# A shorter prologue in a fused mLSTM and MLP-mixer kernel: 40-row products without fills, a split gate computation, and two late subtractions moved back

## The chip, the cores and the metric

The kernel runs on one core of a Trainium2 chip. The metric is the device time of one execution in microseconds (us); the time before the change is the median of three runs. A difference is later told from no change at about 0.2% of it.

## The reference

The kernel computes an mLSTM attention and feeds its output to an MLP-mixer. Shapes: 4 batches, 8 heads, 768 steps, head dimension 40, so 320 features. Cut to what matters:

```python
for t in range(S):                                     # mLSTM, per batch and head
    m_new = maximum(f[t] + m, i[t])
    f_stab, i_stab = exp(f[t] + m - m_new), exp(i[t] - m_new)
    C = f_stab * C + i_stab * outer(v[t], k[t])
    n = f_stab * n + i_stab * k[t]
    y[t] = sigmoid(o[t]) * (C @ q[t]) / maximum(abs(n @ q[t]), 1)
x = y laid out as (batch, 768, 320)
u = x + (relu(x^T @ w_tok1) @ w_tok2)^T                # tokens: 768 -> 256 -> 768
out = u + relu(u @ w_ch1) @ w_ch2                      # channels: 320 -> 1536 -> 320
```

## The kernel before, in words

**Chunks.** The recurrence is computed in chunks: each batch has six chunks of 128 steps, and a unit `(b, c)` is one chunk of one batch for all eight heads. `u0`, `u1`, `u2` are the first three units of batch 0. Within a unit, `st_s` (L308) forms the products k q of every head (16 matmuls, four per head pair of tiles; keys and queries of a head lie in 40 of 64 rows of the tile `raw`, two heads one above the other), `st_p` (L319) multiplies them by the decay factors `dd` on VectorE, `st_pv` (matmuls at L442, or L411 for batches 2 and 3) multiplies them with the values, and `st_state` (from L370) adds what the state `Cst` gives (L380: state times the scaled queries `q3t`) and forms the next state: `pu` (L388) on TensorE, masked with `bm_t` (L393) and added to the decayed state (`Cn`, L397) on VectorE. The tile `raw` exists three times; `zero_rows` (L211) writes zeros once into the 24 unused rows of each 64, since the products of all units but the first read 64 rows.

**Gates.** `gates_of(c0, c1)` (L118) runs the stabiliser's scans for all batches over the chunks c0 to c1 on VectorE, then two subtractions that leave `b_t` and `phi` in the tile `z`. `split` (L175, L176) cuts `z` into bf16 pieces that TensorE spreads over 128 partitions (`spread_split`, `spread_phi`: L166, L181, L184) and over the queries' layout (`spread_q`: L199, L139, L140); ScalarE takes the exponentials (`prep_exp` L292, `prep_q3` L275), and GpSimd or VectorE multiplies the queries by their factors (`prep_q3`, L281). `prep_kw` (L304, GpSimd) scales the keys for the state. `sigmoid` (L222) and `x0_ops` (L479 to L494) finish a unit of batch 0: `x`, and its two-piece form `xh` (ScalarE) and `xl` (GpSimd) for the token GEMM.

**Order.** Nothing is scheduled automatically: each engine executes its instructions in the order in which the program issues them, and so does the queue of loads on SyncE (SP). Batch 0's attention is a prologue that takes the first 48 us or so. From then on TensorE computes the MLP of batch b, and a generator (`att`, L529) is advanced between its steps to issue the attention of batch b+1. In the MLP, `halves` computes the hidden layer of the channel GEMM: ScalarE writes `gh` (L836), VectorE the second piece `gl` (L837). Some hidden tiles lie in a list `closing`; `att` issues their `gh` and `gl` just behind `st_p`.

**Prologue.** `warm(n)` (L897) issues n matmuls on zeros. The order by hand is: loads, `gates_of(0, 2)`, the splits of chunks 0 and 1, the products of `u0`, `gates_of(2, 6)`, the mask (`state_mask`, L104), the products of `u1`, the queries of `u1`, the splits of chunk 2 (VectorE) and of chunks 3 to 5 (GpSimd), the outputs of `u0`; then a loop over c = 1 to 4 prepares unit c+1 (`n1`) and finishes unit c. Two lines of it matter below:

```python
        (nc.vector if u[0] == 1 else nc.gpsimd).tensor_tensor(q3t, q3t, pq, ALU.mult)      # prep_q3, L281
        (v if c == NC - 1 else nc.gpsimd).tensor_tensor(xl, x, f32(xh), ALU.subtract)      # x0_ops, L494
```

Of the kernel before, what the change touches and what calls it, by code (L numbers as in the profile page):

```python
# [18 lines left out]
L = 128  # L19
# [16 lines left out]
def kernel(ctx: ExitStack, tc: tile.TileContext, gates, qk, q3, kv, og,  # L36
# [67 lines left out]
    def state_mask():  # L104
        nc.gpsimd.memset(bm_t, 1.0)
        bm4 = bm_t.rearrange("p (g i e) -> p g i e", g=3, i=3)
        for s in (1, -1):
            nc.gpsimd.affine_select(bm4, bm4, pattern=[[0, 3], [-s * D, 3], [0, E1]], compare_op=ALU.is_ge,
                                    fill=0.0, base=0 if s > 0 else D - 1, channel_multiplier=s)

    floor_b = wp.tile([128, 1], F32, name="floor_b")
    nc.gpsimd.memset(floor_b, 2.0 ** -14 - 0.5)
# [5 lines left out]
    def gates_of(c0, c1):  # L118
        lo, hi = c0 * L, c1 * L
        sl, sd = slice(lo, hi), slice(max(lo, 1), hi)  # L120
        v = nc.vector
        v.tensor_tensor_scan(m_t[:, sl], f_t[:, sl], i_t[:, sl],
                             -1e30 if lo == 0 else m_t[:, lo - 1:lo], op0=ALU.add, op1=ALU.max)
        yield
        first = f_t.rearrange("p (c t) -> p c t", t=L)[:, max(c0, 1):c1, 0]
        v.tensor_tensor(first, first,
                        m_t.rearrange("p (c t) -> p c t", t=L)[:, max(c0, 1) - 1:c1 - 1, L - 1], ALU.add)
        yield
        v.tensor_tensor_scan(phi[:, sd], rst2[:, sd.start - lo:hi - lo], f_t[:, sd],
                             m_t[:, 0:1] if lo == 0 else 0.0, op0=ALU.mult, op1=ALU.add)  # L130
        yield
        v.tensor_tensor(b_t[:, sd], i_t[:, sd], phi[:, sd], ALU.subtract)
        yield
        v.tensor_tensor(phi[:, sd], phi[:, sd], m_t[:, sd], ALU.subtract)
        yield

# [73 lines left out]

    def zero_rows(i):  # L211
        for p in (32, 96):
            t = raws[i][p:p + 32].rearrange("p a h t -> p a (h t)")
            if i == 1:
                nc.scalar.activation(t, zero[p:p + 32].unsqueeze(1).to_broadcast([32, 2, 512]), AF.Copy)
            else:
                nc.gpsimd.memset(t, 0.0)

    def sigmoid(b, r=range(2), part=slice(0, 3)):
# [51 lines left out]
    def prep_q3(u):  # L271
        if u[1] == 0:
            return
        q3t, pq = T[u]["q3"]
        nc.scalar.activation(pq, T[u].get("psq", pq), AF.Exp)  # L275
        if "psw" in T[u]:
            cols_w0_out(T[u]["psw"], u[1])
        if u[1] < NC - 1:
            T[u]["decay"] = a = ap.tile([120, 3], F32, tag="decay", name="decay")
            nc.gpsimd.tensor_copy(a, pq[:, :, L - 1])  # L280
        (nc.vector if u[0] == 1 else nc.gpsimd).tensor_tensor(q3t, q3t, pq, ALU.mult)  # L281

# [24 lines left out]

    def st_s(u, mult=True, mid=iter(()), rows=64, pool=(ps_s, "s")):  # L308
        t = T[u]
        t["s"] = [pool[0].tile([128, 4, L], F32, tag=pool[1], name="ps_sc") for _ in range(2)]  # L310
        for h in range(4):
            for hf in range(2):
                r = t["raw"][64 * hf:64 * hf + rows]
                nc.tensor.matmul(t["s"][hf][:, h, :], r[:, 1, h, :], r[:, 0, h, :], start=True, stop=True)  # L314
        if mult:
            st_p(u, mid)
# [158 lines left out]
    def x0_ops(u):  # L475
# [16 lines left out]
        xh, xl = (pool.tile([128, DM], F32R, tag=a, name=a, bufs=3 if pool is sp else 2) for a in ("xh", "xl"))  # L492
        nc.scalar.activation(xh, x, AF.Copy)
        (v if c == NC - 1 else nc.gpsimd).tensor_tensor(xl, x, f32(xh), ALU.subtract)  # L494
        xs[u] = (x, xh, xl)
# [29 lines left out]
    def after(u, n):  # L525
        i = units.index(u) + n
        return units[i] if i < len(units) else None

    def att(b):  # L529
        for c in range(NC):  # L530
# [14 lines left out]
            st_p(u)  # L545
            while closing:
                closed.append(halves(side.pop(closing.pop())))
            if n2 and not ahead:
# [14 lines left out]
            if not th or joined(u):  # L563
                st_state(u, banks(u))
            if n1 and three(u):
                prep_mask(n1)
# [337 lines left out]

    warm(10)
    zero_rows(1)
    zero_rows(2)
    load_qk(u0, 0)
    load_qk(u0, 1)
    load_kv(u0)  # L910
    for u in us[0:3]:
        load_phi(u)
    load_qk(u1, 0)
    load_qk(u1, 1)
    load_sig(0, 0)
    q3s = {u1: load_q3t(u1)}
    load_kv(u1)
    load_sig(0, 1)

    T[u0]["phi"] = r = [spread_late(ps_h, "h") for _ in range(2)]  # L920
    warm(4)
    step(gates_of(0, 2), 9)
    split(0, 1)
    spread_phi(r, 0)
    t = ps_m.tile([128, HP], F32, tag="m", name="gw")
    cols_w0(t, 0)
    st_s(u0, mult=False, rows=D)
    split(1, 2)
# [5 lines left out]
    prep_kw(u0)  # L934
    state_mask()
    load_qk(u2, 0)
    load_qk(u2, 1)
    q3s[u2] = load_q3t(u2)
    load_kv(u2)
# [8 lines left out]
    step(gr, 9)  # L948
    zero_rows(0)
    load_phi(us[3])  # L950
    load_qk(us[3], 0)
    load_qk(us[3], 1)
    prep_q3(u1)
    prep_kw(u1)
    split(2, 3)
    split(3, NC, nc.gpsimd)
# [6 lines left out]
    st_p(u1)  # L963
    warm(1, (ps_h, "h"))
    spread_split(u2)
# [8 lines left out]
    for c in range(1, NC):  # L974
# [12 lines left out]
        if c < NC - 1:  # L987
            spread_q(n1)
            prep_q3(n1)
            prep_kw(n1)  # L990
        if c == NC - 2:
# [26 lines left out]
        if c < NC - 1:  # L1018
# [6 lines left out]
            else:  # L1025
                dec_abs(nxt[1] + 2)
        step(x0, 9)
        if c == NC - 1:
# [195 lines left out]
```

## Time and profile before

| | us |
|---|---|
| median of three runs (lowest, highest) | 424.73 (424.26, 424.93) |
| the profiled execution, its own time | 424.44 |
| its span from first to last instruction | 422.7 |
| TensorE (PE) busy | 416.2, 98% of the span |
| VectorE (DVE) busy | 277.5, 66% |
| ScalarE (ACT) busy | 185.4, 44% |
| GpSimd (POOL) busy | 143.3, 34% |
| TensorE's granted clock | 1.0 of full speed over the whole span |

Times in the rows are from the start of the span. PE is the matmuls, PEld the weight loads, which run beside them. A row of the timeline that holds several instructions has the time from the first's start to the last's end, and a bracket at its end gives idle time of the engine and what released it. The ends of matmuls are modelled and overlap the next one's start, so gaps are best read from the starts.

### The profile page before, as it was taken

The numbers are of one execution on the slowest core, as the hardware profiler recorded it, in microseconds if no ns is written. First come the engines' busy times: TensorE is split into PE (matmuls) and PEld (weight loads), VectorE is DVE, ScalarE is ACT, GpSimd is POOL, SyncE is SP. The second block draws the span as 40 slices with busy tenths as digits, with TensorE's granted clock in tenths as the row PEclk, the third lists the DMA queues.
The fourth block names the chain that finished last, engine by engine and source line by source line (L and its number), as shares of the span: only waits on it lengthen the run. The fifth ranks groups of instructions, "written<-read, shape, count | busy, mean of one in ns | idle before, by whom it ended". The sixth has DMA issues, their size and how long they took to land.

```text
span 422.7 us, 8990 instructions
## 1 busy us (share of the span) xinstructions
PE 416.2 (98%) x3507; PEld 394.4 (93%) x3507; DVE 277.5 (66%) x617; ACT 185.4 (44%) x431; POOL 143.3 (34%) x188
## 2 busy tenths in 40 slices
PE   8999999999999999999999999999999999999996
PEld 4888989999999999999999999999999999998996
DVE  7988565515868598698696698689786647111412
ACT  4977569893555544234333446234244112111211
POOL 7968488751444412142242220331450110000000
PEclk9999999999999999999999999999999999999999
DMA  7997758941777514344346122443320000000100
GB/s 202 295 299 251 259 171 289 281 142 47 241 212 229 194 34 120 107 118 132 98 151 195 48 78 57 125 116 103 111 86 33 0 32 2 0 0 2 37 27 31
DMA packets 24574, 52.34 MB, mean 124 GB/s; under 512 B 2565, under 2 KB 13325, under 8 KB 24533
## 3 DMA queue, kind: packets, MB, share of 16 engines
q1 hardware_dynamic: 24293, 51.61, 39.2%
q8 instruction: 27, 0.44, 0.4%
q10 hardware_dynamic: 240, 0.18, 0.2%
q14 instruction: 14, 0.11, 0.1%
HBM read 47.73 MB, written 4.04 MB: 122 GB/s over the span
## 4 chain that ended last, share of the span: by engine, by line
PE 93%; DVE 4%; POOL 1%; issue 1%; ACT 1%; DVEq 0%; POOLq 0%
PE acc L703 30%; PE ps_h L824 20%; PE ps_h L850 11%; PE ps_sc L314 5%; PE ps_b L703 5%; PE ps_a L703 5%; PE po L442 4%; PE po L411 3%; PE pu L388 2%; PE po L418 2%; PE po L380 2%; PE warm L897 1%; PE ps_t L771 1%; PE ps_t L770 1%; PE ps_t L769 1%; PE ps_phi L181 1%
## 5 line engine op out<-in xcount | busy, mean ns | idle before, releaser
L824 PE MATMUL ps_h<-uT,c1h 128*128 128x256 f32 x480 | 91.4, 282 | 0.0
L703 PE MATMUL acc<-c2h,gh 128*128 128x320 f32 x288 | 89.0, 318 | 0.0
L836 ACT ACTIVATE gh<-ps_h 128x512 fp32r<-128x512 f32 x48 | 28.6, 597 | 136.2 <-PE ps_h L824 111.7
L703 PE MATMUL acc<-c2l,gh 128*128 128x320 f32 x288 | 86.4, 309 | 0.0
L824 PEld LDWEIGHTS ps_h<-uT,c1h 128*128 128x128 f32 x480 | 75.8, 188 | 0.5
L824 PE MATMUL ps_h<-uT,c1l 128*128 128x256 f32 x256 | 66.1, 281 | 0.0
L703 PE MATMUL acc<-c2h,gl 128*128 128x320 f32 x288 | 61.8, 309 | 0.0
L837 DVE SCALAR_TENSOR_TENSOR gl<-ps_h,gh 128x512 fp32r<-128x512 f32 x48 | 33.0, 688 | 41.8 <-ACT gh L836 41.5
L703 PEld LDWEIGHTS acc<-c2h,gh 128*128 128x128 f32 x288 | 54.1, 188 | 1.4
L703 PEld LDWEIGHTS acc<-c2l,gh 128*128 128x128 f32 x288 | 54.2, 188 | 0.9
L854 DVE SCALAR_TENSOR_TENSOR gl<-ps_h,gh 128x512 fp32r<-128x512 f32 x24 | 16.6, 692 | 49.1 <-ACT gh L853 49.1
L824 PEld LDWEIGHTS ps_h<-uT,c1l 128*128 128x128 f32 x256 | 48.3, 189 | 0.0
L461 POOL TENSOR_TENSOR sig<-sig,ht 128x320 f32<-128x320 f32 x18 | 14.7, 818 | 98.7 <-DVE ht L422 90.6
L703 PEld LDWEIGHTS acc<-c2h,gl 128*128 128x128 f32 x288 | 47.2, 188 | 0.0
L295 ACT ACTIVATE dd<-dd,bcol 128x128 f32<-128x128 f32 x144 | 45.8, 392 | 1.4 <-POOL dd L285 1.3
L850 PE MATMUL ps_h<-uT,c1h 128*128 128x512 f32 x120 | 36.0, 394 | 0.0
L324 DVE TENSOR_TENSOR dd<-ps_sc,dd 128x512 f32<-128x512 f32 x48 | 30.9, 682 | 7.6 <-PE ps_sc L314 7.5
L512 POOL TENSOR_TENSOR xl<-x,xh 128x320 fp32r<-128x320 f32 x18 | 15.8, 876 | 51.2 <-DVE xh L510 49.8
L853 ACT ACTIVATE gh<-ps_h 128x512 fp32r<-128x512 f32 x24 | 14.3, 594 | 41.2 <-PE ps_h L850 41.2
L314 PE MATMUL ps_sc<-raw 64*128 64x128 f32 (+1 forms) x384 | 26.1, 281 | 0.0
L850 PEld LDWEIGHTS ps_h<-uT,c1h 128*128 128x128 f32 x120 | 22.1, 188 | 3.9
L314 PEld LDWEIGHTS ps_sc<-raw 64*128 64x128 f32 (+1 forms) x384 | 22.9, 188 | 2.5 <-issue 0.8
(154 smaller groups left out, 862.0 us busy)
## 6 DMA issues: line engine op xcount, KB each, us to landing
dd<-phi_d SPq DMA_DIRECT2D x18, 512.0 KB
wst<-in_wc_dram SPq DMA_DIRECT2D x22, 384.0 KB
kvt<-in_kv_dram SPq DMA_DIRECT2D x24, 324.0 KB
raw<-in_qk_dram SPq DMA_DIRECT2D x48, 160.0 KB
sig<-in_og_dram SPq DMA_DIRECT2D x8, 480.0 KB
out_dram<-x SPq DMA_DIRECT2D x24, 160.0 KB
q3t<-in_q_dram SPq DMA_DIRECT2D x20, 180.0 KB
wst<-in_wt_dram SPq DMA_DIRECT2D x8, 384.0 KB
```

Of the source, the lines that this page charges most:

```text
L295: nc.scalar.activation(dd[:, h, :], dd[:, h, :], AF.Exp, bias=bcol[:, c, HP * b + h:HP * b + h + 1])
L314: nc.tensor.matmul(t["s"][hf][:, h, :], r[:, 1, h, :], r[:, 0, h, :], start=True, stop=True)
L324: nc.vector.tensor_tensor(dd, t["s"][hf], dd, ALU.mult)
L442: nc.tensor.matmul(o, t["dd"][:, ROW[h], :], x, start=c == 0 and h == 0, stop=h == H - 1)
L461: nc.gpsimd.tensor_tensor(sg, sg, ht[:, :, 0:D], ALU.mult)
L512: nc.gpsimd.tensor_tensor(xl, x, f32(xh), ALU.subtract)
L703: nc.tensor.matmul(ps, a, m, start=(first and i == 0), stop=(last and i == n - 1))
L824: nc.tensor.matmul(ps[:, j, :], c1[x][:, a:a + 128], u[:, y, :], start=not opened and part is first and i == 0 and (order == 0 and not clo ...
L836: nc.scalar.activation(gh, ps, AF.Relu)
L837: nc.vector.scalar_tensor_tensor(gl, ps, 0.0, f32(gh), op0=ALU.max, op1=ALU.subtract)
L850: nc.tensor.matmul(ps, c1[x][:, a:a + 128], u[:, :, y, :], start=n == 0, stop=n == len(todo) - 1)
L854: nc.vector.scalar_tensor_tensor(gl, ps, 0.0, f32(gh), op0=ALU.max, op1=ALU.subtract)
```

## The change

1. `st_s` reads 40 rows of each half of `raw` instead of 64, for every unit. `zero_rows` is gone with its six fills (two on ScalarE, four on GpSimd).
2. `state_mask` is issued at the very start of GpSimd's work instead of behind `kw` of `u0`.
3. `warm(4)` becomes `warm(2)`, and the `warm(1)` ahead of the pieces of `u2` is gone.
4. The two subtractions of the gates leave `gates_of` and become `gates_end(c0, c1)`. For chunks 2 to 5 they are issued in two portions: chunk 2 alone, then the split of chunk 2, then the product of `u1`'s queries and factors (now on VectorE), then chunks 3 to 5.
5. Loads: the value load of `u0` goes behind both halves of `raw` of `u1` and the first gate load `sig`; the second `sig` load goes behind both halves of `raw` of `u2`.
6. `x0_ops` yields between `xh` and `xl`. In the loop's pass c = 4 the subtraction `xl` of unit 3 is issued behind the queries' product of unit 5.
7. In `att`, for batches 2 and 3 and c = 0 or 1, the tiles in `closing` are finished behind `prep_p3` and `st_state` instead of behind `st_p`.

The diff, cut to its core:

```diff
+    state_mask()
     floor_b = wp.tile([128, 1], F32, name="floor_b")
...
-        v.tensor_tensor(b_t[:, sd], i_t[:, sd], phi[:, sd], ALU.subtract)
-        yield
-        v.tensor_tensor(phi[:, sd], phi[:, sd], m_t[:, sd], ALU.subtract)
-        yield
+
+    def gates_end(c0, c1):
+        sd = slice(max(c0 * L, 1), c1 * L)
+        nc.vector.tensor_tensor(b_t[:, sd], i_t[:, sd], phi[:, sd], ALU.subtract)
+        nc.vector.tensor_tensor(phi[:, sd], phi[:, sd], m_t[:, sd], ALU.subtract)
...
-        (nc.vector if u[0] == 1 else nc.gpsimd).tensor_tensor(q3t, q3t, pq, ALU.mult)
+        (nc.vector if u[0] == 1 or u == u1 else nc.gpsimd).tensor_tensor(q3t, q3t, pq, ALU.mult)
...
-                r = t["raw"][64 * hf:64 * hf + rows]
+                r = t["raw"][64 * hf:64 * hf + D]
...
         nc.scalar.activation(xh, x, AF.Copy)
+        yield
         (v if c == NC - 1 else nc.gpsimd).tensor_tensor(xl, x, f32(xh), ALU.subtract)
...
             st_p(u)
-            while closing:
-                closed.append(halves(side.pop(closing.pop())))
+            if b == 1 or c > 1:
+                close()
...
                 st_state(u, banks(u))
+            close()
...
     warm(10)
-    zero_rows(1)
-    zero_rows(2)
     load_qk(u0, 0)
     load_qk(u0, 1)
-    load_kv(u0)
...
     load_sig(0, 0)
+    load_kv(u0)
     q3s = {u1: load_q3t(u1)}
     load_kv(u1)
-    load_sig(0, 1)
...
-    warm(4)
+    warm(2)
     step(gates_of(0, 2), 9)
+    gates_end(0, 2)
...
     prep_kw(u0)
-    state_mask()
     load_qk(u2, 0)
     load_qk(u2, 1)
+    load_sig(0, 1)
...
     st_p(u0)
     step(gr, 9)
-    zero_rows(0)
...
+    gates_end(2, 3)
+    split(2, 3)
     prep_q3(u1)
     prep_kw(u1)
-    split(2, 3)
+    gates_end(3, NC)
     split(3, NC, nc.gpsimd)
...
     st_p(u1)
-    warm(1, (ps_h, "h"))
     spread_split(u2)
...
             prep_q3(n1)
+            if c == 4:
+                step(x0, 9)
             prep_kw(n1)
...
-        step(x0, 9)
+        step(x0, 2 if c == 3 else 9)
```

**GpSimd at the start of the prologue.** `sel` is the last piece of the selection matrices, `kw` the scaled keys of `u0` and then of `u1`, `z` the split of chunks 3 to 5. Before:

```order
L102 COPY sel_128<-id_126 128x360
L112 MEMSET floor_b 128x1
L217 MEMSET raw_137 32x1024 x2
L304 TENSOR_TENSOR kw<-kvt,wcol 128x320
L105 MEMSET bm_t 120x369
L108 AFFINE_SELECT bm_t<-bm_t 120x369 x2
L217 MEMSET raw_135 32x1024 x2
L280 COPY decay<-pq 120x3
L281 TENSOR_TENSOR q3t<-q3t,pq 120x384
L304 TENSOR_TENSOR kw<-kvt,wcol 128x320
L175 TENSOR_TENSOR z<-z 9x2x384
```

And now:

```order
L102 COPY sel_128<-id_126 128x360
L105 MEMSET bm_t 120x369
L108 AFFINE_SELECT bm_t<-bm_t 120x369 x2
L113 MEMSET floor_b 128x1
L298 TENSOR_TENSOR kw<-kvt,wcol 128x320
L274 COPY decay<-pq 120x3
L298 TENSOR_TENSOR kw<-kvt,wcol 128x320
L177 TENSOR_TENSOR z<-z 9x2x384
```

The fills and the query product are gone from this engine, and the mask stands ahead of the first `kw`.

**VectorE between the products of `u0` and the output of `u0`** (`dd` is `st_p` of `u0`, `z` the scan, the subtractions and the split, `po` the output of `u0`). Before:

```order
L324 TENSOR_TENSOR dd<-ps_sc,dd 128x512 x2
L129 SCALAR_TENSOR_TENSOR z<-rst,f_t 36x512
L132 TENSOR_TENSOR z<-i_t,z 36x512
L134 TENSOR_TENSOR z<-z,m_t 36x512
L175 TENSOR_TENSOR z<-z 9x2x128
L176 TENSOR_TENSOR z<-z 9x2x128
L479 TENSOR_TENSOR po<-po,sig 128x8x40
```

And now:

```order
L318 TENSOR_TENSOR dd<-ps_sc,dd 128x512 x2
L130 SCALAR_TENSOR_TENSOR z<-rst,f_t 36x512
L136 TENSOR_TENSOR z<-i_t,z 36x128
L137 TENSOR_TENSOR z<-z,m_t 36x128
L177 TENSOR_TENSOR z<-z 9x2x128
L178 TENSOR_TENSOR z<-z 9x2x128
L275 TENSOR_TENSOR q3t<-q3t,pq 120x384
L136 TENSOR_TENSOR z<-i_t,z 36x384
L137 TENSOR_TENSOR z<-z,m_t 36x384
L473 TENSOR_TENSOR po<-po,sig 128x8x40
```

The split of chunk 2 moves up by most of the subtractions, and three instructions stand between it and the output of `u0`.

**VectorE in unit (2, 1)**, the first of two such places (the second is unit (3, 1); `r` and `p` are the second and third pieces of the products, `pu` and `Cn` the state). Before:

```order
L324 TENSOR_TENSOR dd<-ps_sc,dd 128x512 x2
L837 SCALAR_TENSOR_TENSOR gl<-ps_h_2409,gh 128x512
L343 TENSOR_TENSOR r<-dd 128x512 x2
L351 TENSOR_TENSOR p_2459<-r 128x512 x2
L393 TENSOR_TENSOR pu<-pu,bm_t 120x246
L393 TENSOR_TENSOR pu<-pu,bm_t 80x82
L397 SCALAR_TENSOR_TENSOR Cn<-Cn,decay,pu 120x123 x2
L397 SCALAR_TENSOR_TENSOR Cn<-Cn,decay,pu 80x82
L837 SCALAR_TENSOR_TENSOR gl<-ps_h_2444,gh 128x512
```

And now:

```order
L318 TENSOR_TENSOR dd<-ps_sc,dd 128x512 x2
L337 TENSOR_TENSOR r<-dd 128x512 x2
L345 TENSOR_TENSOR p_2447<-r 128x512 x2
L387 TENSOR_TENSOR pu<-pu,bm_t 120x246
L387 TENSOR_TENSOR pu<-pu,bm_t 80x82
L391 SCALAR_TENSOR_TENSOR Cn<-Cn,decay,pu 120x123 x2
L391 SCALAR_TENSOR_TENSOR Cn<-Cn,decay,pu 80x82
L837 SCALAR_TENSOR_TENSOR gl<-ps_h_2401,gh 128x512
L837 SCALAR_TENSOR_TENSOR gl<-ps_h_2436,gh 128x512
```

The first `gl` now stands behind `Cn`, next to the second. TensorE's order is unchanged in the whole program but for the three `warm` matmuls.

## Rows read from the trace of the kernel before

**Rows 1.** The page's part 1: busy time, share and instructions of TensorE.

```profile
PE 416.2 (98%) x3507; PEld 394.4 (93%) x3507; DVE 277.5 (66%) x617; ACT 185.4 (44%) x431; POOL 143.3 (34%) x188
```

**Rows 2.** Waits of PE and PEld: who waited for whom, us in total, times, longest.

```profile
PE po L411 <- DVE Cn L397: 0.7, 2, 0.4
...
PEld po L380 <- POOL q3t L281: 0.6, 1, 0.6
```

**Rows 3.** Timeline of PE, 6 to 26 us: start, us, engine, line, operation.

```profile
6.49 1.40 PE L897 MATMUL warm<-zero 128*128 128x512 bf16 x4
7.72 0.39 PE L181 MATMUL ps_phi<-z,id 128*128 128x128 bf16 x4
...
15.00 0.38 PE L897 MATMUL warm<-zero 128*128 128x512 bf16 x1
15.22 0.38 PE L166 MATMUL ps_phi<-late_b,id_b 128*128 128x512 bf16 x1
16.29 0.39 PE L181 MATMUL ps_phi<-z,id 128*128 128x128 bf16 x4 [0.69 <-DVE z L176]
...
18.57 0.38 PE L199 MATMUL ps_q<-z,sel 128*120 128x128 bf16 x3
...
25.55 0.77 PE L388 MATMUL pu<-kvt,kw 128*120 128x123 f32 x6
```

**Rows 4.** Groups by line and form, PE: the products; busy us, mean ns.

```profile
L314 PE MATMUL ps_sc<-raw 64*128 64x128 f32 x368 | 24.9, 280 | 0.0
...
L314 PE MATMUL ps_sc<-raw 40*128 40x128 f32 x16 | 1.2, 285 | 0.0
```

**Rows 5.** Tile z on VectorE: duration ns min/median/max, first and last start.

```profile
L175 DVE TENSOR_TENSOR z<-z x3: 417/586/1267, 5.8 to 14.1; 9x256 f32<-9x256 f32 x3
L176 DVE TENSOR_TENSOR z<-z x3: 418/419/829, 6.4 to 15.4; 9x256 f32<-9x256 f32 x3
L132 DVE TENSOR_TENSOR z<-i_t,z x2: 415/549/683, 4.9 to 12.7; 36x255 f32<-36x255 f32 x1, 36x512 f32<-36x512 f32 x1
```

**Rows 6.** Timeline of POOL, 5 to 17 us, and at 40 us.

```profile
6.23 1.95 POOL L217 MEMSET raw<- 32x1024 f32 x2
9.18 0.72 POOL L304 TENSOR_TENSOR kw<-kvt,wcol 128x320 f32<-128x320 f32 x1 [1.01 <-ACT wcol L143]
...
10.33 1.25 POOL L108 TENSOR_SCALAR_AFFINE_SELECT bm_t<-bm_t 120x369 f32<-120x369 f32 x2
...
14.09 1.00 POOL L281 TENSOR_TENSOR q3t<-q3t,pq 120x384 f32<-120x384 f32 x1
15.06 0.90 POOL L304 TENSOR_TENSOR kw<-kvt,wcol 128x320 f32<-128x320 f32 x1
...
40.04 1.02 POOL L281 TENSOR_TENSOR q3t<-q3t,pq 120x384 f32<-120x384 f32 x1
```

**Rows 7.** Timeline of DVE, 10 to 25 us, and `q3t` at 135 us.

```profile
10.00 1.29 DVE L324 TENSOR_TENSOR dd<-ps_sc,dd 128x512 f32<-128x512 f32 x2 [0.74 <-PE ps_sc L314]
...
16.27 0.50 DVE L479 TENSOR_TENSOR po<-po,sig 128x320 f32<-128x320 f32 x1
...
24.19 0.49 DVE L488 TENSOR_TENSOR x<-po,den 128x320 f32<-128x320 f32 x1
...
134.91 0.56 DVE L281 TENSOR_TENSOR q3t<-q3t,pq 120x384 f32<-120x384 f32 x1
```

**Rows 8.** Timeline of DVE and then of PE, 173 to 179 us.

```profile
173.54 0.69 DVE L837 SCALAR_TENSOR_TENSOR gl<-ps_h,gh 128x512 fp32r<-128x512 f32 x1 [0.47 <-ACT gh L836]
...
177.37 0.80 DVE L397 SCALAR_TENSOR_TENSOR Cn<-Cn,decay,pu 120x123 f32<-120x123 f32 x3
...
178.22 0.20 PE L411 MATMUL po<-v,dd 128*128 128x82 bf16 x1 [0.35 <-DVE Cn L397]
```

**Rows 9.** Timeline of ACT, 13 to 19 us.

```profile
13.73 1.90 ACT L222 ACTIVATE sig<-sig 128x960 f32<-128x960 f32 x2
...
16.94 1.24 ACT L292 ACTIVATE dd<-ps_phi 128x512 f32<-128x512 f32 x2
```

More of the change, by code (lines that the diff above doesn't have):

```diff
@@ L209 @@
     raws = [ap.tile([128, 2, 4, L], F32, tag=f"raw{i}", name=f"raw{i}", bufs=1) for i in range(3)]
[L211 to L217, printed above, removed]
     def sigmoid(b, r=range(2), part=slice(0, 3)):
@@ L306, in prep_kw, with st_s @@
         t["kw"] = kw
-    def st_s(u, mult=True, mid=iter(()), rows=64, pool=(ps_s, "s")):
+    def st_s(u, mult=True, mid=iter(()), pool=(ps_s, "s")):
         t = T[u]
@@ L527, in after, with close @@
         return units[i] if i < len(units) else None
+    def close():
+        while closing:
+            closed.append(halves(side.pop(closing.pop())))
     def att(b):
@@ L926 @@
     cols_w0(t, 0)
-    st_s(u0, mult=False, rows=D)
+    st_s(u0, mult=False)
     split(1, 2)
```

## The prediction

> **What bounds the kernel now.** I read the busy times first: TensorE works 416.2 of 422.7 us [rows 1], so the end moves only by what TensorE no longer waits for or no longer does. Next I read whom it waits for [rows 2]. Past the start there are three such places: a state `Cn` from VectorE, twice; a query product from GpSimd in the prologue; and a split from VectorE, which the timeline shows at 16.29 us [rows 3]. That is all there is to win here, some 2.5 us. A change can also lose, by making a wait where there is none. So I cost each edit at its place, in the order of time, and then look for what is late next.
>
> The sum is made against the profiled execution, 424.44, which lies 0.29 under the median of 424.73. That is inside the spread of the runs, and I add it back at the end.
>
> **40-row products.** Before the change one unit already reads 40 rows and 23 read 64: 285 against 280 ns mean [rows 4]. The number of rows does not set the time, so 23 x 16 products cost what they did: 0. The fills stood on GpSimd (1.95 us for two [rows 6], twice) and on ScalarE, where neither engine was waited for; taking them out is worth 0 by itself. What it does is let the loads of `raw` go out without waiting for them.
>
> **Early stretch, TensorE's side.** Of the four `warm` matmuls at 6.49 two go. The one at 15.00 has its successor at 15.22, so a matmul of this form takes 0.22: the pieces of `u0` start 2 x 0.22 = 0.43 earlier than 7.72 (half of the four, (7.72 - 6.49)/2 = 0.62, is the upper bound) [rows 3]. They need the split of chunk 0, which ended at 6.44 + 0.42 = 6.86 [rows 5]. The third `warm`, 15.00 to 15.22, goes too, and with the 0.43 the pieces of `u2` could start some 0.43 + 0.22 earlier plus the whole stall in front of 16.29. TensorE would be at them at about 14.9.
>
> **Early stretch, VectorE's side.** TensorE then has VectorE as its next bound, and the question is by how much (d) VectorE's output of `u0`, at 16.27 [rows 7], shifts. From there on VectorE works without a pause up to the output `x` of `u1`, at 24.19 + 0.49 = 24.68, and TensorE's `pu` at 25.55 [rows 3, 7] overwrites a bank that `x` of `u1` reads. With 0.06 for the signal that leaves 0.81 - d for TensorE's gain in this stretch: whatever it wins before, it must wait there for `x`.
>
> The terms of d. First the rows show how VectorE and GpSimd get in each other's way: the split's first half takes 0.42 alone and 1.27 when it begins at 14.10, just behind the start of GpSimd's query product at 14.09, and it ends 0.28 behind that product's end; its second half takes 0.83 instead of 0.42 beside `kw` [rows 5, 6]. So an instruction of two SBUF inputs stands still until GpSimd's ends. Beside the fills at 6.23 the second half took its least, 0.42 [rows 5, 6].
> - The mask, moved to about 6.6, now lies beside the splits of chunks 0 and 1 and the first scan. Its two selects take 1.25 together [rows 6]. Bounds 0 (each falls in a gap) and 1.25 (VectorE stands through both); half and a little more, since one split is under way when the first select asks: +0.75.
> - `kw` of `u0` (0.72 [rows 6]) waited for ScalarE; 0.43 earlier it meets the last small addition of the gates in front of 10.00. Bounds 0 (its values, now loaded later, are not there yet) and 0.72; half: +0.35.
> - Against both stands the pause of 0.74 in front of 10.00 [rows 7], which absorbs as much: -0.74. Sum so far +0.36.
> - The query product of `u1`: 0.56 on VectorE [rows 7]: +0.59 with the gap behind it.
> - Two more subtractions. A subtraction of 512 took 0.68 and one of 255 took 0.42 [rows 5], so 0.16 is fixed: 2 x 0.16 = +0.32.
> - No query product on GpSimd beside the split, and `kw` no longer beside its second half: 1.27 + 0.83 - 2 x 0.42 = -1.26 [rows 5].
> - `kw` of `u1`, 0.90 [rows 6], comes earlier and falls on some other gate instruction: 0 to 0.7, half +0.35.
>
> d = 0.36 + 0.59 + 0.32 - 1.26 + 0.35 = **+0.36**, bounds -0.9 and +1.4 when all ends fall together. TensorE's gain in the early stretch is then 0.81 - 0.36 = **0.45**. Its ends: 1.4, where TensorE's own earliest start is the limit, and -0.6.
>
> The Trainium skill, "SBUF — State Buffer", section "Who interferes with whom", states that a VectorE instruction with two SBUF inputs contends with a GpSimd instruction that reads SBUF, not with one that only writes it, and that the later one blocks fully. The rows on the product, `kw` and the fills agree. By that rule alone this part of the change is a bad trade: fills that hinder nobody are replaced, beside the splits, by selects that read and block; with the full 1.25 in place of 0.75 d is 0.86 and the early gain nothing. The mask has no instruction of VectorE beside it in the rows that fixes the price, so I keep half.
>
> **The loads moved.** The values of `u0` go behind four loads of `raw` and one of the gates; they are first needed by `kw` of `u0` at 9.18, with slack behind it, and the term above has their being late in its lower bound. The second gate load goes behind `raw` of `u2`. Its user is the second half of the two sigmoids at 13.73, which ends at 15.63 [rows 9]; behind them on ScalarE stand the exponentials of `u2`. I take it as just in time: 0; late is a rival below.
>
> **Queries ahead of `xl`.** In front of 41.11 TensorE waited 0.57 for the product that GpSimd began at 40.04 [rows 2, 6], right behind `xl`. Now the product goes first. It can start when its factors are there, about 0.5 us earlier, and TensorE then meets the state `Cn` of `u4`, which is no earlier than before. I take **0.45**, bounds 0.1 and 0.57. `xl` now ends behind the product; it is next needed by the token GEMM soon after, with little to spare, which is the lower bound.
>
> **`gl` behind the pieces.** At 178.22 TensorE waited for `Cn`, which began at 177.37 [rows 8], and so once more a batch later, 0.7 us of wait in two times [rows 2]; with the weight load that cannot run ahead the matmuls come 0.5 later each. The 0.69 of `gl` at 173.54, and the 0.47 that VectorE idled for `gh` in front of it [rows 8], leave this chain: `Cn` comes at least 0.69 earlier, the wait was under that, so it goes. `gl` itself now ends where the second `gl` of the stretch ends, still ahead of its matmuls, which TensorE reaches only behind all of L411 and the state's products. **1.0** for the two, bounds 0.9 and 1.06. What is late next there is nothing that the rows show.
>
> **Sum.** 0.45 + 0.45 + 1.0 = 1.9 against 424.44: 422.54. With the 0.29 up to the median: **422.8 us**, 0.45% below 424.73.
>
> **Rivals.**
> 1. VectorE is not held up (the values of `u0` land late, or the selects fall in gaps): d is -0.4 or so, TensorE's early gain 1.2 and the sum 2.6: 422.1. For it speaks that nothing in the rows shows a select beside a split; against it that GpSimd's readers did block wherever they met one [rows 5]. Chance 0.21.
> 2. VectorE is held up by all of both selects and by `kw`: d of 0.85 to 1.1, early gain 0 to -0.3, sum 1.3: 423.4. This is the case that the rule of the Trainium skill on the two engines, above, makes of the selects. Half of their price stands between it and mine. Chance 0.17.
> 3. No change that can be told (a difference under 0.2%, 0.85 us): the early stretch loses its 0.6 and `xl` or the moved `gl` gives half of its gain back at a wait that the rows don't show: 424.1. Chance 0.09.
> 4. Slower, by one load: the second `sig`, now behind two more loads of `raw`, lands at X. ScalarE stands in its queue until then, and behind it are half the sigmoids (0.95), the 1.31 of its table change up to 16.94, and the first exponential of `u2` (0.62) [rows 9]; TensorE's `ps_q`, at 18.57 [rows 3], needs the bank that this frees. It comes at X + 0.95 + 1.31 + 0.62 + 0.06 = X + 2.94. Up to X = 15.6 that costs nothing; the other gains, 1.45, are eaten at X = 17.1; over 0.85 slower from X = 17.9, say 425.8. Against it speaks that the queue ahead of this load no longer waits for fills, so that all of it goes out earlier. Chance 0.04.
> 5. Forty rows lose what lets two products, one above the other, overlap: if each took twice its pitch, a unit would take about 1 us more, 23 us in all. The one unit that had 40 rows did not [rows 4]. Chance 0.02: 440 or more.
>
> My forecast has the rest, 0.47.
>
> **Range and chances.** The forecast's own bounds with ordinary ends are 422.2 to 423.4. To hold 8 in 10 the range takes in rival 1 down to an early gain of 1.4 with the upper bounds of the others (3.0: 421.7) and rival 2 and part of rival 3 up to 424.1. Faster by over 0.2% (below 423.88): forecast, rival 1 and most of rival 2, 0.83. Within: rival 3 and the rest, 0.12. Slower: rivals 4 and 5 with their neighbours, 0.05.
>
> **What would show it.** Right: the wait for the split in front of 16.29 gone, a new wait of a few tenths of us on VectorE or none near `pu` of `u2`; no wait for a query product at 41 us; no wait on `Cn` at L411, twice; 16 products of 40 rows still 1.1 us. Wrong: a wait of ScalarE on a gate load near 14 us, splits of chunk 0 or 1 of over a microsecond, or a new wait on `xl` or `gl` in the list.

## The result and the profile after

The changed kernel takes **426.85 us** (median of 8 runs, 425.42 to 428.58), the kernel before 424.17 in the same session (8 runs, 423.60 to 425.29). The ratio is 1.0061, 95% interval 1.0036 to 1.0087: 0.6% slower, where 422.8 us and 0.45% faster were forecast. The profiled execution took 425.80 us, with a span of 424.1; it is one of the quicker ones of the eight, whose mean granted TensorE clock lay between 0.988 (428.58 us) and 0.996. In the profiled execution of the kernel before it was 1.0.

TensorE is busy about as long as before [rows 1], with three matmuls fewer, so the time has to be looked for in its waits and in its clock:

```profile
PE 416.6 (98%) x3504; PEld 395.7 (93%) x3504; DVE 280.3 (66%) x620; ACT 183.1 (43%) x429; POOL 138.4 (33%) x183
```

The list of PE's waits after the change (in total, times, longest) has none of the three waits past the start that the prediction named, and a new long one:

```profile
PE ps_q L201 <- ACT dd L286: 2.7, 1, 2.7
PE warm L897 <- POOL zero L61: 1.4, 1, 1.4
PE po L405 <- DVE p L345: 0.2, 1, 0.2
```

TensorE's timeline there, against [rows 3]: the pieces of `u2` start at 14.31 instead of 16.29, without a wait for the split. Then the queries of `u2` come at 19.35 instead of 18.57, and the instructions behind them need far longer than they did.

```profile
14.31 0.39 PE L183 MATMUL ps_phi<-z,id 128*128 128x128 bf16 x4
...
15.51 1.16 PE L308 MATMUL ps_sc<-raw 40*128 40x128 f32 x16
19.35 0.33 PE L201 MATMUL ps_q<-z,sel 128*120 128x128 bf16 x3 [2.68 <-ACT dd L286]
...
19.57 1.33 PE L374 MATMUL po<-Cn,q3t 120*128 120x164 f32 x6
20.70 1.36 PE L382 MATMUL pu<-kvt,kw 128*120 128x123 f32 x6
21.85 2.67 PE L436 MATMUL po<-kvt,dd 128*128 128x82 f32 x16
24.36 0.38 PE L168 MATMUL ps_phi<-late_b,id_b 128*128 128x512 bf16 x1
...
43.08 0.92 PE L374 MATMUL po<-Cn,q3t 120*128 120x164 f32 x6
```

ScalarE's timeline says what TensorE waited for. Where it ran both sigmoids in one stretch before [rows 9], the second now waits 2.56 us for its load:

```profile
12.82 1.00 ACT L216 ACTIVATE sig<-sig 128x960 f32<-128x960 f32 x1
16.38 1.00 ACT L216 ACTIVATE sig<-sig 128x960 f32<-128x960 f32 x1 [2.56 <-DMA sig<-in_og_dram]
17.40 1.28 ACT L286 ACT_TABLE_LOAD   x1
18.70 1.09 ACT L286 ACTIVATE dd<-ps_phi 128x512 f32<-128x512 f32 x2
```

And the windows of 1 us (busy time of PE, PEld, DVE, ACT, POOL with their counts, then the granted clock, the DMA share and GB/s) say why the rest is slow: after the stop the clock is at 0.50, its lower level of 1.2 GHz, for some 3.4 us.

```profile
18.00:19.00 1.00, 0.00 (x0) 0.00 (x0) 0.78 (x2) 0.99 (x2) 0.83 (x1) 1.00 0.90 294
19.00:20.00 1.00, 0.65 (x8) 0.65 (x8) 0.67 (x2) 1.00 (x3) 0.00 (x0) 0.96 1.03 268
20.00:21.00 1.00, 1.00 (x7) 1.00 (x6) 0.62 (x2) 1.00 (x5) 0.72 (x1) 0.50 1.10 315
...
23.00:24.00 1.00, 1.00 (x9) 1.00 (x9) 1.00 (x4) 0.00 (x0) 0.00 (x0) 0.83 0.97 337
```

But for the three `warm` matmuls, TensorE's instructions stand in the same order in both programs, so the two traces can be compared start by start. The lead is 1.97 us at 16.29 of before; the stop turns it into a lag of 0.78, the low clock into one of 2.35 (24.36 against 22.01). The product at 41.11 comes at 43.08: 0.38 won by the queries ahead of `xl`. At L411 (L405 after the change) in units (2, 1) and (3, 1) about 0.5 is won each, 0.5 is lost again between them on a wait for the pieces `p` near 193 us, and at the end the lag is 1.36, the difference of the spans (424.1 and 422.7 in the rounded figures).

### The profile page after: what moved, and what is told of

It is laid out like the page before. It is cut to its first block, busy times and chain, and to the rows that moved or that the text cites. A ratio compares the mean times of both kernels' runs of the same rounds, so it can differ in the third digit from the quotient of the medians.

```text
span 424.1 us, 8972 instructions
## 1 busy us (share of the span) xinstructions
PE 416.6 (98%) x3504; PEld 395.7 (93%) x3504; DVE 280.3 (66%) x620; ACT 183.1 (43%) x429; POOL 138.4 (33%) x183
## 4 chain that ended last, share of the span: by engine, by line
PE 91%; DMA 3%; DVE 3%; ACT 1%; SPq 0%; issue 0%; DVEq 0%
PE acc L703 29%; PE ps_h L824 19%; PE ps_h L850 11%; PE ps_sc L308 5%; PE ps_a L703 5%; PE ps_b L703 5%; PE po L436 5%; PE pu L382 3%; PE po L405 3%; DMA sig<-in_og_dram 2%; PE po L374 2%; PE po L412 2%; DMA raw<-in_qk_dram 1%; PE ps_t L771 1%; PE ps_t L769 1%; PE ps_t L770 1%
## 5 line engine op out<-in xcount | busy, mean ns | idle before, releaser
L455 POOL TENSOR_TENSOR sig<-sig,ht 128x320 f32<-128x320 f32 x18 | 14.7, 818 | 98.0 <-DVE ht L416 89.4
L308 PE MATMUL ps_sc<-raw 40*128 40x128 f32 x384 | 26.1, 280 | 0.0
L308 PEld LDWEIGHTS ps_sc<-raw 40*128 40x128 f32 x384 | 22.9, 187 | 2.6 <-issue 0.8
```

What stands on the lines that cost most here:

```text
L455: nc.gpsimd.tensor_tensor(sg, sg, ht[:, :, 0:D], ALU.mult)
```

## The experiments

The theory after the result: the gate load's place stops ScalarE, that stops TensorE, and the stop costs the clock. The rivals: VectorE's new order or other loads would have stopped the prologue too; the low clock belongs to the work and not to the stop. All medians stand against the kernel before in the same session, with the ratio's 95% interval.

**The gate load back in its place** (on the changed kernel).

```diff
     load_kv(u1)
+    load_sig(0, 1)
...
     load_qk(u2, 1)
-    load_sig(0, 1)
```

> The changed kernel with one line moved: the second gate load is issued ahead of both loads of raw of unit u2 again, as before the change. Theory (the load's place is the whole loss): the load lands by about 13.6 us, the second sigmoid follows the first with no wait, TensorE has no wait at the queries of u2 and no stretch at half clock. TensorE's stall of 2.7 us and the 1.6 us lost to the clock go, at most capped by the output of u1; against the kernel before it is then faster by 1.9 to 2.9 us: 421.3 to 422.3 where the kernel before has 424.2. Rival (VectorE's new order or the moved values of u0 hold the prologue up as well): the wait moves to another releaser in the stretch of 14 to 26 us and the kernel stays above 423.5.

Measured 424.53 us (422.33 to 427.24) against 424.32; ratio 1.0003 (0.9980 to 1.0026). 2.3 us of the loss are gone, but the time is not where the theory put it (421.3 to 422.3): the rival is right as well. The profiled execution took 426.79, one of the longer ones. In it the gate load, in its old place, still comes late: ScalarE's second sigmoid starts at 15.62, after a wait of 1.73 us. `raw` of `u2`, now behind the gate load, stops TensorE by 0.66 and 0.62 us, and the clock falls all the same. It is low from 20 to near 27 us, over which TensorE falls back by another 3.3 us. Two executions took 422.33, with mean clocks of 0.998 and 1.0; that nothing stopped TensorE in them is only likely, since they have no trace.

```profile
PE ps_sc L308 <- DMA raw<-in_qk_dram: 1.3, 2, 0.7
```

```profile
20.00:22.00 2.00, 2.00 (x13) 2.00 (x12) 0.77 (x3) 1.16 (x3) 2.00 (x4) 0.52 1.00 267
22.00:24.00 2.00, 2.00 (x11) 2.00 (x11) 1.86 (x6) 1.08 (x2) 0.16 (x1) 0.50 1.03 242
```

**TensorE kept busy over the stop** (on the changed kernel).

```diff
         if c < NC - 1:
+            if c == 1:
+                warm(12)
             spread_q(n1)
```

> The changed kernel with 12 matmuls on zeros put on TensorE in front of the queries of u2, where it stands for 2.7 us. They write a bank that nobody reads. Theory (the clock falls because TensorE stands): the wait for ScalarE ends where it did, near 19.35 us, but the granted clock stays at 1.0 from 20 to 24 us, the state's products of u1 and u2 have their former pitch, and the kernel is 1.6 us faster than the changed one: about 425.2 where the changed one has 426.8. Rival (the fall belongs to the work behind the wait, not to the standing): the clock falls to 0.5 as before and the time is within 0.4 us of the changed kernel.

424.88 us (424.59 to 425.56) against 424.32; ratio 1.0008 (0.9996 to 1.0020): 2.0 us faster than the changed kernel, though the load came at 16.90 here and the zeros delayed the queries to 20.34. Of the stop 0.8 us is left, in front of the zeros. The clock stays up; the windows' lines:

```profile
18.00:20.00 2.00, 2.00 (x11) 0.94 (x10) 1.44 (x4) 1.99 (x3) 1.34 (x1) 1.00 0.87 279
20.00:22.00 2.00, 2.00 (x21) 1.80 (x20) 1.13 (x2) 1.91 (x6) 1.20 (x3) 1.00 0.99 244
```

So the low clock follows from standing and not from the work behind it, and it is the larger part of the loss: 2.0 of 2.7 us, with the queries 1.0 us later than in the changed kernel.

**The gate load moved alone** (on the kernel before).

```diff
     load_kv(u1)
-    load_sig(0, 1)
...
     load_qk(u2, 1)
+    load_sig(0, 1)
```

> The kernel before with only the second gate load moved behind both loads of raw of u2. Theory: it lands some 1 to 2.5 us later than the 13.7 us of before, ScalarE waits for it, and TensorE's queries of u2 come at landing + 2.95 us instead of 18.57; with a landing of 16 us that is a wait of about 0.4 us or more, and the time is between equal and 2 us above the kernel before, the upper end if the clock falls. Rival (the move hurts only together with the earlier start of everything else, since there the loads are also issued in another order): no wait of ScalarE for a load beyond 0.3 us and no difference.

425.43 us (424.35 to 425.77) against 424.32; ratio 1.0017 (1.0005 to 1.0029): 1.1 us by the medians, 0.7 by the ratio. As in the theory, ScalarE's sigmoid starts at 16.84, TensorE waits 1.2 us for what is behind it, and the queries of `u2` come 1.2 us later than in [rows 3]. The clock holds, though TensorE had waited another 1.17 us shortly before, for the split:

```profile
16.84 1.00 ACT L222 ACTIVATE sig<-sig 128x960 f32<-128x960 f32 x1 [2.61 <-DMA sig<-in_og_dram]
```

```profile
16.27 0.39 PE L181 MATMUL ps_phi<-z,id 128*128 128x128 bf16 x4 [1.17 <-DVE z L176]
...
19.81 0.33 PE L199 MATMUL ps_q<-z,sel 128*120 128x128 bf16 x3 [1.18 <-ACT dd L292]
```

```profile
20.00:22.00 2.00, 2.00 (x23) 2.00 (x20) 1.48 (x3) 2.00 (x7) 1.25 (x3) 1.00 1.02 236
```

**The closing tiles back behind the products** (with the gate load put back).

```diff
-            if b == 1 or c > 1:
-                close()
+            close()
```

> The second gate load in its old place, and in addition the closing tiles finished behind the products of the unit again, as before the change. If the move of the subtraction gl is worth what the rows of before gave, TensorE waits for the state twice again, near 177 and 275 us, 0.5 us of matmul time each, and this is 1.0 us slower than the kernel with the gate load alone put back. Rival: the move only shifts the wait to another piece, and the two are the same.

One execution, 423.47 us. That is not above the 424.53 of the run with the gate load alone put back, as was expected; that run spreads over 5 us, so one execution settles nothing on the time. What the trace shows is the waits: TensorE's two waits for the state are there again, and between 132 us and the end its lead over the kernel before grows no more (1.16 and 0.99 us):

```profile
PE po L405 <- DVE Cn L391: 0.9, 2, 0.5
```

**Another order of loads** (as the first, and the values of `u1` behind `raw` of `u2`).

```diff
-    load_kv(u1)
+    load_sig(0, 1)
...
     load_qk(u2, 1)
-    load_sig(0, 1)
+    load_kv(u1)
```

> The changed kernel with another order of loads only: the second gate load ahead of raw of u2 again, and the values of u1 (324 KB), which are not needed before about 17 us, behind raw of u2. Theory (from 6 to 16 us the DMA engines are full, and the changed kernel asks for the second gate load and raw of u2 2 us sooner than they can come): both land about 1 us sooner than with the gate load alone put back, ScalarE waits under 0.5 us, TensorE is not stopped for more than 0.5 us and its clock stays at 1.0; median 421 to 422.5 with a narrow spread. Rival (the order does not matter, the prologue is short of loads by the same amount in any order): the wait goes to kw and pu of u1, the clock falls again in most runs, and the median stays at 424 or above.

424.11 us (423.11 to 427.21) against 424.46; ratio 1.0004 (0.9986 to 1.0023): a miss, the theory had 421 to 422.5. The first stop is gone: both sigmoids in one stretch, a lead of 2.04 us at the pieces of `u2`. But at 29 us TensorE is 0.5 behind. 0.5 of the lead goes up to the queries of `u2`, 0.9 at the products of `u3` and 1.1 at the pieces of unit 4. What it met last is ScalarE waiting for weights, with the work of unit 4 in its queue behind them:

```profile
26.09 0.52 ACT L661 ACTIVATE pf<-wst 128x384 f32<-128x384 f32 x1 [2.58 <-DMA wst<-in_wt_dram]
```

**No second sigmoid** (on the changed kernel).

```diff
-    sigmoid(0)
+    sigmoid(0, [0])
```

> The changed kernel without the second of ScalarE's two sigmoids of batch 0, all loads as in the changed kernel. It leaves out the sigmoid of the output gates of chunks 3 to 5 of batch 0. Theory (ScalarE's queue behind that one load is the whole stop): no wait of TensorE for the exponentials of u2, clock 1.0, and all of the 2 us that TensorE has gained by the pieces of u2 stay: 421 to 422.3. Rival (raw of u2, the values or VectorE stop the prologue just the same): TensorE waits there for another releaser and the time stays above 423.5.

423.78 us (422.74 to 427.82) against 424.46; ratio 0.9986 (0.9966 to 1.0006). 3.1 us under the changed kernel, and still above 423.5, on the rival's side: `raw` of `u3` stops TensorE for 0.9 in front of 22.96 us, and ScalarE waits 1.63 for weights in front of 20.37.

**The second sigmoid deferred** (on the changed kernel).

```diff
     load_kv(u2)
+    load_sig(0, 1)
...
-    sigmoid(0)
+    sigmoid(0, [0])
...
             prep_exp(n2, 1)
+        if c == 2:
+            sigmoid(0, [1])
```

> The changed kernel with the second gate load behind the values of u2 and its sigmoid taken out of the prologue's start and put behind the exponentials of unit 4 (pass c = 2 of the loop), which costs ScalarE two more table loads of 1.28 us there. Theory: as without the sigmoid in the start, unless ScalarE is short of time between 25 and 40 us, where it was busy for 83%: 421 to 422.5, or up to 1.5 more if the weights' pieces come late. Rival as for the run without the sigmoid.

428.51 us (427.86 to 430.21) against 424.46; ratio 1.0098 (1.0075 to 1.0121). A miss: at the new place ScalarE has no 3.5 us to spare, TensorE waits 2.6 in front of 37.29 us, and the clock is at 0.50 from 39 to 48 us.

**The gates whole again** (with the new order of loads; `u1`'s query product on GpSimd).

```diff
-    gates_end(2, 3)
-    split(2, 3)
+    gates_end(2, NC)
     prep_q3(u1)
     prep_kw(u1)
-    gates_end(3, NC)
+    split(2, 3)
```

> The new order of loads, and the gates as before the change: both subtractions over chunks 2 to 5 at once, u1's query product on GpSimd, the split of chunk 2 behind it. If the splitting of the gates is what brings the pieces of u2 forward, they start near 15.5 to 16 us again instead of 14.3, with a wait of TensorE for z of 1 us or so, and the kernel is 0.5 to 1 us slower than with the new order alone. Rival (the loads alone set the pace of this stretch): no difference over 0.3 us.

423.68 us (422.05 to 428.44) against 424.46; ratio 0.9979 (0.9962 to 0.9996). The pieces of `u2` start at 15.61, after a wait of 0.6 for the split, as the theory had it, where the new order alone has them at 14.25. But the kernel is no slower than with the gates split: the lead that the split gives is not what sets the time.

**The late edits alone** (on the kernel before: of the diff, the yield behind `xh`, the two steps of `x0`, and `close()` as the change has it).

> The kernel before with edits 6 and 7 alone: xl behind the query product of unit 5, and gl behind the pieces in two chunks. The prologue's loads, gates, fills and warm matmuls are as before. Theory (the changed kernel's loss lies in the first 24 us alone, its late edits give what the rows said): TensorE waits neither at 41 us nor for the state at L411, 0.3 to 0.45 and twice 0.5 us are gained, no half clock; 1.3 to 1.45 us faster than the kernel before: about 423.0 where that has 424.4, with its narrow spread. Rival (the gain is eaten by a later wait): less than 0.7 us faster.

**422.68 us** (422.55 to 424.45) against 424.74; ratio 0.9955 (0.9937 to 0.9973). The best of the versions that do all the work, and better than forecast for it. PE's waits are down to the prologue's:

```profile
PE ps_phi L181 <- DVE z L176: 1.4, 2, 1.2
PE warm L903 <- POOL zero L61: 1.4, 1, 1.4
```

**40 rows and no fills alone** (on the kernel before).

```diff
-                r = t["raw"][64 * hf:64 * hf + rows]
+                r = t["raw"][64 * hf:64 * hf + D]
...
-    zero_rows(1)
-    zero_rows(2)
...
-    zero_rows(0)
```

> The kernel before with edit 1 alone: 40 rows in every product, no fills. Theory: the products keep their 280 ns, the loads of raw go out without waiting, TensorE's waits stay where they were: no change within 0.5 us. Rival (fewer rows cost, or the earlier loads of raw push others back): over 0.5 us slower, seen as longer products or as a wait for a load in the first 30 us.

426.83 us (424.56 to 431.18) against 424.74; ratio 1.0041 (1.0015 to 1.0067). Slower, as the rival had it, but by a way that neither had. Without fills in between, GpSimd's query product, `kw` and split start sooner and fall on VectorE's subtractions and split, which then wait for them. GpSimd's timeline, and VectorE's:

```profile
12.14 1.00 POOL L273 TENSOR_TENSOR q3t<-q3t,pq 120x384 f32<-120x384 f32 x1
13.15 1.13 POOL L296 TENSOR_TENSOR kw<-kvt,wcol 128x320 f32<-128x320 f32 x1
14.96 1.63 POOL L175 TENSOR_TENSOR z<-z 9x768 f32<-9x768 f32 x1 [0.69 <-DVE z L134]
```

```profile
12.20 1.50 DVE L132 TENSOR_TENSOR z<-i_t,z 36x512 f32<-36x512 f32 x1
13.72 1.09 DVE L134 TENSOR_TENSOR z<-z,m_t 36x512 f32<-36x512 f32 x1
14.85 0.42 DVE L175 TENSOR_TENSOR z<-z 9x256 f32<-9x256 f32 x1
15.30 1.57 DVE L176 TENSOR_TENSOR z<-z 9x256 f32<-9x256 f32 x1
```

The subtractions took 0.68 before [rows 5]. TensorE's wait for the split is 1.9 us instead of 0.7. The profiled execution (425.39) has a clock of 0.999; in 7 of the 10 the mean clock is 0.996 or less, and these are the longer ones.

**40 rows with the fills kept**, and **fills aside** (as that, but written to tiles of their own, so that no load waits for them).

```diff
-            t = raws[i][p:p + 32].rearrange("p a h t -> p a (h t)")
+            t = other[i][p:p + 32]
```

> The kernel before with 40 rows in every product and all fills kept; nothing needs the fills any more, but the loads of raw of u1, u2 and u3 wait for them as before. Theory (edit 1 costs because the loads go out sooner and the stream of loads behind comes later or less evenly, not because of the rows): as the kernel before, 424.5 with its narrow spread, and 2 us under the run with 40 rows and no fills (426.8). Rival (the 40-row products cost it): 426 to 427 with the same wide spread.

> As the run before this, but the fills go to tiles of their own (960 of 1024 columns, in pieces of 320): ScalarE and GpSimd do the same work, and no load waits for it. Theory (holding the loads back is what the fills did): 426 to 427 with a wide spread and some stretches at half clock, as with 40 rows and no fills. Rival (the work of the fills on the two engines held something back, not the loads): 424.5, as the kernel before.

424.29 us (423.67 to 425.60) and 424.94 us (423.48 to 425.75) against 424.60; ratios 0.9996 (0.9983 to 1.0008) and 1.0002 (0.9988 to 1.0017). The rows cost nothing, as forecast. In the second the theory fell, the rival is right: it was the fills' time on the engines, not their holding of the loads. (ScalarE's fill is kept too; that GpSimd's are the ones that count is read from the traces.) With the fills (2.42 us in pieces) ahead of it the query product starts at 14.89, behind VectorE's split, which is undisturbed. GpSimd's timeline, and VectorE's:

```profile
12.26 2.42 POOL L220 MEMSET other<- 32x320 f32 x6
...
14.89 1.00 POOL L284 TENSOR_TENSOR q3t<-q3t,pq 120x384 f32<-120x384 f32 x1
```

```profile
13.48 0.42 DVE L175 TENSOR_TENSOR z<-z 9x256 f32<-9x256 f32 x1
13.93 0.42 DVE L176 TENSOR_TENSOR z<-z 9x256 f32<-9x256 f32 x1
```

**480 KB less to load** (new order of loads, without the second gate load; ScalarE's second sigmoid works on the first tile again).

```diff
-    load_sig(0, 1)
+    sig[(0, 1)] = sig[(0, 0)]
...
-    sigmoid(0)
+    sigmoid(0, [0, 0])
```

> The changed kernel with the new order of loads (values of u1 behind raw of u2) and without the second gate load of batch 0, 480 KB; ScalarE runs its second sigmoid on the first gate tile again, so that its time stays. It leaves out the gates of chunks 3 to 5 of batch 0. Theory (from 6 to about 30 us the stream of loads sets the pace, whatever waits for it): everything behind comes 1.6 us sooner, ScalarE does not wait 2.6 us for weights near 26 us, and TensorE keeps at least 1.2 of the 2.0 us it is ahead at the pieces of u2: median 421 to 422.5. Rival (after the first stop it is ScalarE's or VectorE's own work that uses up the lead): TensorE falls back to the times of before by 30 us just the same, and the median is that of the new order, 424.1, or within 0.7 of it.

422.76 us (422.13 to 423.29) against 424.74; ratio 0.9946 (0.9925 to 0.9968), narrow, and just above the theory's 421 to 422.5. TensorE keeps 1.1 of a lead of 1.9 us past 27 us, where the new order alone was 0.5 behind, and ScalarE's wait for weights is half as long:

```profile
24.57 0.53 ACT L661 ACTIVATE pf<-wst 128x384 f32<-128x384 f32 x1 [1.26 <-DMA wst<-in_wt_dram]
```

**Two first loads from ScalarE's queue** (new order of loads).

```diff
-    load_sig(0, 0)
-    load_kv(u0)
+    load_sig(0, 0, nc.scalar)
+    load_kv(u0, nc.scalar)
```

> The changed kernel with the new order of loads, and the first gate load and the values of u0 issued from ScalarE's queue, which stands idle then, instead of from SyncE's. Theory (the stream of loads sets the pace, and from 3 to 6 us the DMA engines moved 0.2 MB per us against 0.3 later, for want of issued loads): the stream gets 0.2 to 0.3 MB ahead, and TensorE with it: 0.5 to 1 us faster than the new order alone, about 423.3. Rival (the engines are slow in that stretch for the shape of the loads, not for want of them): no difference over 0.4 us.

424.17 us (422.64 to 429.95) against 424.74; ratio 0.9980 (0.9959 to 1.0001). A miss: it can't be told apart from the new order alone.

**Loads, fills, rows and mask as before** (edits 3, 4, 6 and 7 alone).

> Edits 3, 4, 6 and 7 alone: fills, 64 rows, mask and the order of loads as before the change, with the gates split, the three warm matmuls gone and the two late edits. Theory (the stream of loads leaves about half a us): the pieces of u2 come 1 us or more sooner than before, and most of that is given back by 30 us at raw of u3 or at the weights; 422.2 to 422.9, at most 0.5 us under the late edits alone (422.7), or above them where the wait lowers the clock. Rival (the stream has room when the loads are held as before): the whole lead is kept: 421.5.

423.45 us (421.75 to 425.30) against 424.60; ratio 0.9974 (0.9957 to 0.9992), above the 422.2 to 422.9 of the theory. The pieces of `u2` come 1.41 us sooner than before, the lead is 0.57 at 28 us, after a wait of ScalarE for weights of 1.22 us at 25.08. So the prologue's edits add nothing to the late ones, which alone give 0.9955, even when nothing stops TensorE early.

## Why the prediction was wrong

**The loads moved.** This step failed: "I take it as just in time: 0". The load came at 16.38. Rival 4 had the mechanism, and its formula, X + 2.94 = 19.32, met the queries of `u2` at 19.35. The prediction's own sign of being wrong, a wait of ScalarE on a gate load near 14 us, is there as well. The rival got a chance of 0.04, because the queue ahead of the load would go out earlier. For the issue that came true: SyncE issues the load at 7.57, against 7.40 before and 8.22 where the load alone was moved. But ScalarE could use it only at 16.38, 8.8 us after the issue, where before it was there by 14.7 at the latest. Timelines of SP, before and after:

```profile
7.40 0.44 SPq L55 DMA_DIRECT2D sig<-in_og_dram  x1
```

```profile
7.57 0.40 SPq L55 DMA_DIRECT2D sig<-in_og_dram  x1
```

The stream of loads had little room. Before the change it moved 314 GB/s from 10 to 14 us and 285 from 14 to 18, at DMA shares of 1.06 and 0.94; after it 298 and 285, at 1.05 and 0.84. At that rate two loads of `raw` ahead, 320 KB, are some 1.1 us (an estimate). And the gate load put back in its old place, issued at 6.79, still came at 15.62: the changed kernel asks for it sooner, and it does not come sooner.

**The price of a stop.** By the rival's own scale X = 16.38 should have cost 0.78 and left a gain of 0.7. The trace agrees so far: TensorE is 0.78 behind at the queries. What was left out is the clock: the stop of 2.68 us was followed by 3.4 us at half clock, which cost 1.6 us in the profiled execution and 2.0 in the median by the run that kept TensorE busy. In the profiled execution with the gate load put back, two waits of 0.66 and 0.62 us were followed by a longer stretch at half clock, which cost 3.3. No row of before shows the clock fall; the longest wait there past the start is 0.69 us.

**Early stretch.** The forecast lead of 0.45 was too low and beside the point. VectorE's d came out at -0.65 instead of +0.36: the output of `u0` starts at 15.62 against 16.27. All of that was won ahead of the products of `u0`, which start at 9.35 against 10.00; from there to the output both kernels take 6.27 us, as the forecast's terms had it in sum (+0.59, +0.32, -1.26 and +0.35 give 0), though not one by one. TensorE's own start was mis-sized too: the pieces of `u0` come 0.90 earlier, beyond the bound of 0.62. Part of that is the execution: with the prologue of before up to there, they come at 7.72 in the profiled execution of before, at 7.23 with the gate load moved alone and at 6.58 with the late edits alone, and the pieces of `u2` at 16.29, 16.27 and 15.64. So of the lead of 1.97, up to some 0.65 need not be the change's. `kw` of `u0` came late (the lower bound) and the mask cost about 0.46 of the 0.75. In VectorE's timeline after, the second half of the split of chunk 1 takes 0.69 beside the selects where 0.42 is its least [rows 5], and the scan behind it 1.47 where it took 1.28 before:

```profile
7.05 0.69 DVE L178 TENSOR_TENSOR z<-z 9x256 f32<-9x256 f32 x1
7.77 1.47 DVE L123 TENSOR_TENSOR_SCAN m_t<-f_t,m_t,i_t 36x512 f32<-36x512 f32 x1
...
13.67 0.97 DVE L275 TENSOR_TENSOR q3t<-q3t,pq 120x384 f32<-120x384 f32 x1
...
15.62 0.48 DVE L473 TENSOR_TENSOR po<-po,sig 128x320 f32<-128x320 f32 x1
```

The selects beside them on GpSimd took 1.47 us, 0.22 more than before [rows 6]:

```profile
6.71 1.47 POOL L108 TENSOR_SCALAR_AFFINE_SELECT bm_t<-bm_t 120x369 f32<-120x369 f32 x2
```

TensorE's lead reached 1.97 us, and no run that loads everything was more than 0.65 ahead at 30 us: the late edits alone kept their 0.65, the closing tiles put back 0.60 of 1.06, the loads as before 0.57 of 1.41. With another order of loads the lead was gone by then, with 480 KB less half of it stayed. The cap that I took, the output of `u1` on VectorE, was not the one that decided. The run with less to load points to the stream of loads; of the three places where the new order lost its lead, the trace puts only the last on a load. The full price of the selects (rival 2) did not come: VectorE lost 0.46 beside them, and not 1.25.

**Fills: 0 on the path.** Failed where they go alone: that costs 2.1 us in the median, 0.95 in the profiled execution, whose clock held. The fills' time had kept GpSimd's reading instructions off VectorE's gates. Whether the whole change pays for it is not shown. Its query product is on VectorE, where `kw` of `u1` beside it goes with 0.97 us instead of 0.56 [rows 7]; but the run with the gates whole has that product on GpSimd again, without fills, its subtractions take 1.03 and 1.52, and it is no slower.

**40 rows.** Right: 280 ns before and after, and 424.29 against 424.60 with the fills kept.

**Queries ahead of `xl`.** Right: 0.38 in the trace against 0.45.

**`gl` behind the pieces.** Right: about 0.5 twice, and the run that undoes it has the waits again. Not foreseen: 0.5 lost near 193 us in the profiled execution, where a GpSimd select of 1.29 us, tied to a load, fell on VectorE's `r` (2.17 us for two). It belongs to that execution: of the ten other traces with this edit, eight lose nothing there and two lose 0.1 and 0.2.

What stays open: why the late edits alone gain 2.06 in the median where the steps sum to 1.45 and the traces show 1.3 (its profiled execution was also 0.65 ahead early on), and how the 4.7 us between the late edits alone (2.06 under the kernel before) and the whole change (2.68 over it) divide. The moved gate load alone costs 1.1 (0.7 by the ratio), the clock 2.0. Why the clock fell after waits of 0.66 and 0.62 us and held through two of 1.2 us is open too. That the rest comes of each edit taking slack that covered another was only argued.

## What to carry to other kernels

When a stall of one engine is taken out, look at what the loads do at the same time: if the DMA engines are full there, the engine only comes sooner to a load that doesn't. Here another order of loads moved the wait on; fewer bytes removed part of it. Price a stop of TensorE with the clock that it may lose, not with its length alone. And idle or useless work on an engine can be a spacer: before it goes, check which instructions move up into whose way.

## What the runs showed of the hardware

TensorE's clock fell to half some 0.5 us after it resumed from a stop of 2.68 us and stayed there for 3.4 us; it also fell in an execution whose waits there were 0.66 and 0.62 us (0.52 from 20 to 22 us, 0.50 from 22 to 24), and held where the gate load alone was moved, with waits of 1.17 and 1.18 us. Twelve matmuls on zeros over the stop kept it at 1.00. A fill of GpSimd, which only writes, left VectorE's split, an instruction of two SBUF inputs, at its least time (0.42). GpSimd's products, scaled keys and splits, which read, stretched it to 1.27 and 1.57, and the subtractions of 512 columns from 0.68 to 1.50 and 1.09.
